# All sixteen decodes of second-layer weights during the first layer, and the second output layer of group 0 as seven products

## The chip, the core and the metric

The kernel runs on one core of one Trainium2 chip. The metric is device time in microseconds (us) of the whole kernel. Work is shared by TensorE (PE, matrix products), VectorE (DVE), ScalarE (ACT), GpSimd (POOL), and SyncE (SP), which here only issues DMAs, in order, from one queue.

## The reference

All values are float32. Attention without a softmax is followed by a normalisation and by two layers with a hidden dimension:

```
kv  = einsum('bhsd,bhse->bhde', k, v);  o = einsum('bhsd,bhde->bhse', q, kv)      # 8 x 8 heads x 576 x 64
x   = o / sqrt(mean(o*o, -1) + 1e-6) * g_norm          # reshaped to 4608 tokens x 512
x   = (sigmoid(x @ w_gate) * (x @ w_val)) @ w_out      # 512 -> 1536 -> 512, first layer
h   = x @ w_in                                         # 512 -> 2048, second layer
out = where(h > 0, h, exp(min(h, 0)) - 1) @ w_out2     # 2048 -> 512
```

## The kernel before

Precision. Each float32 factor is split into a high and a low half, and a product of two factors is three matmuls into one PSUM bank (high x high, high x low, low x high). For the activations of an output layer this is `split`: ACT writes the high half (line 725), DVE the low half (line 727), into one of three buffers J.

Tiling. The 4608 tokens are six groups of two blocks of 384. For every group in turn the first layer runs its input stage (gate and value products) and its output stage; the attention of the group after is woven in between. Then for every group in turn the second layer runs its input stage (`in2`, line 846 on) and its output stage. Results of the first layer wait in DRAM (x2d).

Seven products. A product of 2 x 2 blocks is done as seven block products instead of eight, on sums and differences of blocks, with additions of PSUM banks into SBUF afterwards. `quad` does that for input stages. For the output stage of the second layer there are two functions: `out2_plain` keeps six PSUM banks and streams 512 columns per matmul; `out2` makes the differences T1, T2, T3 of the input blocks (`combine`, line 891, on POOL, the last of each on DVE; T4 on DVE), runs seven products of 256 columns per matmul (lines 916 to 918) and adds up on DVE (line 930). Group 0 takes `out2_plain`, the other five `out2`. The T buffers of `out2` ("w") lie in the memory of the buffers raw, wk and kv.

Weights. The second layer's weights arrive in a packed form and are decoded on the chip, sixteen times (eight pairs of tiles for the input layer, "I", eight for the output layer, "O"). A decode loads two raw tiles (line 359, 512 KB each), makes words on ACT (lines 362, 364) and DVE (366, 370), builds four sums on POOL (378 to 381) in a buffer sf, splits both into halves (ACT 385, DVE 386), and stores the pieces to DRAM (wsI, wsO; lines 395 and 398). All later products read these pieces into five buffers S of 1 MB. Twelve decodes run in the first layer, as the tuple `DEC` deals them to groups 0 to 5; the four that are left run in group 0 of the second layer, marked `late`. A late decode takes its sf from the three kv buffers, which until group 5 of the first layer hold the attention's k and v loads (line 499); the others take it from the four wk buffers.

Order. All work is written down as tasks with dependencies. The order on PE is that of the program; the orders on DVE, ACT, POOL and SP come from a planner (`Plan`), which places tasks by due times and tries random variations from a seed. Engines then run their lists in order, so a row that waits holds up all rows behind it.

Of the kernel before, what the change touches and what calls it, by code (L numbers as in the profile page):

```python
# [32 lines left out]
WARM = 7  # L33
IDLE = (8, 8, 20, 40)
LAG = 4.0
DEC = (0,2,3,3,2,2)
SEVEN = (1,2,3,4,5)


# [25 lines left out]
class Plan:  # L65
# [16 lines left out]
    def add(self, eng, dur, fn, after=(), bufs=(), due=None, queue=None):  # L82
        t = Task(eng, dur, fn, after, bufs, due, len(self.tasks))
        for d in t.after:
            d.next.append(t)
        self.tasks.append(t)
        if eng == "PE":
            (self.pe if queue is None else queue).append(t)
        return t
# [22 lines left out]

    def run(self):

        tries, now, rand = [], 0.0, random.Random(3)
        for t in self.pe:
            t.started, now = now, now + t.dur
        cuts = [0] + self.marks + [len(self.pe)]

        def one(times, bias={}):  # L120
            for t in self.tasks:
                t.bias = bias.get(t, 0.0)
            for t, x in zip(self.pe, times):
                t.started = x
            if len(self.round()) < len(self.tasks):
                return times
            got = [t.started for t in self.pe]
            end = max(t.started + t.dur for t in self.pe)
            tries.append((end, times, got, [(got + [end])[b] - got[a] for a, b in zip(cuts, cuts[1:])], bias, [t.started for t in self.tasks]))
            return got  # L130

        times = [t.started for t in self.pe]
        for n in range(self.ROUNDS):
            got = one(times)
            times = [(x + y) / 2 for x, y in zip(times, got)] if n % 2 else got
        for n in range(self.MIXES):
            mixed, at = [], 0.0
            for k, (a, b) in enumerate(zip(cuts, cuts[1:])):
                r = min(tries, key=lambda r: r[3][k])
                wide = rand.choice((0.0, 0.5, 1.5, 4.0, 8.0)) if n else 0.0  # L140
                mixed += [x - r[1][a] + at + rand.uniform(-wide, wide) for x in r[1][a:b]]
                at += r[3][k]
            one(sorted(mixed))
        busy = [sum(t.dur for t in self.pe[a:b]) for a, b in zip(cuts, cuts[1:])]
        for n in range(self.STEPS):
            best = min(tries, key=lambda r: r[0])
            k = rand.choices(range(len(busy)), [x - y + 0.3 for x, y in zip(best[3], busy)])[0]
            a, b = cuts[k], cuts[k + 1]
            if n % 3:
                lo, hi = (best[2] + [best[0]])[a] - 5.0 if k else 0.0, (best[2] + [best[0]])[b]  # L150
                wide, bias = rand.choice((1.0, 3.0, 8.0)), dict(best[4])
                for t, x in zip(self.tasks, best[5]):
                    if t.eng != "PE" and lo <= x < hi and rand.random() < 0.08:
                        bias[t] = rand.uniform(-wide, wide) if rand.random() < 0.8 else 0.0
                one(best[1], bias)
                continue
            other = rand.choice(sorted(tries, key=lambda r: r[3][k])[:8]) if n % 2 else best
            wide = rand.choice((0.3, 1.0, 3.0, 6.0))
            shift = (best[2] + [best[0]])[a] - (other[2] + [other[0]])[a]
            now = [x + shift + rand.uniform(-wide, wide) for x in other[1][a:b]]  # L160
            one(sorted(best[1][:a] + now + best[1][b:]), best[4])
        for t in self.tasks:
            t.bias = min(tries, key=lambda r: r[0])[4].get(t, 0.0)
        for t, x in zip(self.pe, min(tries, key=lambda r: r[0])[1]):
            t.started = x
        order = self.round()
        assert len(order) == len(self.tasks)
        return order
# [123 lines left out]
def tile_kernel(ctx: ExitStack, tc: tile.TileContext, kv, kvtail, qt, g2, w1, w2, out):  # L292
# [5 lines left out]
    plan = Plan()  # L298
# [51 lines left out]
    def decode(layer, fp, after=None, late=False):  # L350

        src, idx = (w1, "gvo".index(layer)) if layer in "gvo" else (w2, "IO".index(layer))
        order = (2 * fp, 2 * fp + 1) if layer in "oO" else (2 * fp + 1, 2 * fp)
        k = "3" if late else "2" if layer in "IO" else ""
        wh, wp = plan.buf("wk", "wh" + k), plan.buf("wk", "wp" + k)
        word = []
        for n, f in enumerate(order):
# [4 lines left out]
            a = add("ACT", 0.57, lambda raw=raw, n=n: nc.scalar.activation(  # L362
                wh.slot[:, n, :], raw.slot[:, :, 1].bitcast(F32), AF.Copy, scale=2.0 ** -112), [ld], [raw, wh])
            b = add("ACT", 0.57, lambda raw=raw, n=n: nc.scalar.activation(
                wp.slot[:, n, :].bitcast(I32), raw.slot[:, :, 0].bitcast(U32), AF.Copy, scale=0.93 * 2.0 ** -29), [ld], [raw, wp])
            c = add("DVE", 0.61, lambda raw=raw, n=n: nc.vector.scalar_tensor_tensor(
                wp.slot[:, n, :].bitcast(I32), raw.slot[:, :, 1], -(2 ** 31), wp.slot[:, n, :].bitcast(I32),
                op0=ALU.bitwise_and, op1=ALU.bitwise_or), [b], [raw, wp])
# [3 lines left out]
            op0=ALU.logical_shift_left, op1=ALU.bitwise_or), word, [wh, wp])  # L372
        if layer in "IO":
            d = ws2[fp] if layer == "I" else wo2[:, :, fp]
            sf = plan.buf("kv", "kv", "q a c n -> q a (c n)") if late else plan.buf("wk", "sf")
            A = lambda i: (wh.slot[:, i // 2, i % 2 * 256:i % 2 * 256 + 256] if layer == "I" else wh.slot[:, i % 2, i // 2 * 256:i // 2 * 256 + 256])
            T = lambda i: sf.slot[:, i // 2, i % 2 * 256:i % 2 * 256 + 256]
            s1 = add("POOL", 0.72, lambda: nc.gpsimd.tensor_tensor(T(0), A(0), A(1), op=ALU.add), [w], [wh, sf])
# [460 lines left out]
    def load_x2(g, blk):  # L839
        res = []  # L840
        for m in range(NCC):
            f = plan.buf("v", "xf")
            res.append((f, dma(P * BLK * 4, lambda f=f, m=m: nc.sync.dma_start(out=f.slot, in_=x2d[g][:, blk, m, :]), [x2_there[g, blk, m]], [f], early=40.0)))
        return res
# [153 lines left out]
    n = len(plan.tasks)  # L998
# [8 lines left out]
    for fp in range(2):  # L1007
        dec[fp] = decode("g", fp) + decode("v", fp)
    rate[0] = 340e3
    hs = [{} for _ in range(NF1 // 2)]  # L1010
# [31 lines left out]
    for fp in range(NF1 // 2):  # L1042
        dec[fp] = decode("o", fp)
    w2_pairs = [(c, fp) for c in "IO" for fp in range(NF2 // 2)]
    for g in range(NG):
        if g:
# [3 lines left out]
            hs = [in1(fp, X, done, fresh if g == 1 else stream) for fp in range(NF1 // 2)]  # L1050
# [3 lines left out]
        n = len(plan.pe)  # L1054
        plan.marks.append(n)
        (out1_products if g in SEVEN else out1)(g, hs)
        if g:
            m = DEC[g]
            a, b = n if g == 1 else start + 30, n - 20 if g > 1 else len(plan.pe) - 20
# [4 lines left out]
    for g in range(NG):  # L1064
        plan.marks.append(len(plan.pe))
        X, done = sides(load_x2(g, 0), load_x2(g, 1), "DVE")
        n = len(plan.pe)
        hs = [in2(fp, X, done) for fp in range(NF2 // 2)]
        if g == 0:
            m = len(w2_pairs)  # L1070
            for k in range(m):
                decode(*w2_pairs.pop(0), after=plan.pe[n + int((len(plan.pe) - n) * (0 + (0.8 - 0) * k / m))], late=True)
            gate = add("POOL", 0.05, lambda: None, [t for t in plan.tasks if any(b.cls in ("raw", "wk", "kv") for b in t.bufs)])
        (out2 if g else out2_plain)(g, hs)

    for t in plan.run():
        t.fn()
# [31 lines left out]
```

## Time and profile before

| | |
|---|---|
| median of 3 runs | 1631.77 us (1631.62 to 1632.13) |
| profiled execution, own time | 1632.44 us |
| its span, first to last instruction | 1630.7 us |
| PE busy | 1617.9 us, 99% of the span |
| DVE busy | 1197.0 us, 73% |
| ACT busy | 854.6 us, 52% |
| POOL busy | 427.4 us, 26% |
| DMA moved | 495.27 MB, mean 304 GB/s |
| granted TensorE clock | 1.0 in the mean |

The busy share of an engine is an average over stages. Matmuls are pipelined, their records overlap, and a busy PE need not stream at its peak; the length of a stage over its count of matmuls says what one costs. An idle time is put down to the releaser that came last. "SPq" rows are DMAs that SP issues. A DMA's share is the mean busy share of the core's 16 DMA engines.

### The profile page before, as it was taken

Reading aid. Unit: us, or ns where it says so; the run is one execution under the profiler, and the core shown is the slowest. Engines: PE = TensorE matmul, PEld = TensorE weight load, DVE = VectorE, ACT = ScalarE, POOL = GpSimd, SP = SyncE. Lnnn points to the kernel's source line nnn. Section 1 sums busy time; section 2 is a strip of 40 time slices with the busy share of each in tenths; the row PEclk is TensorE's granted clock in tenths of the full one; section 3 lists DMA queues with packets and bytes.
Section 4 is the critical chain, followed back from the end, with each engine's and each line's share of the span. In section 5 each row is a group of like instructions: output and inputs, shape, how many; then the busy total and the mean of one; then the engine's idle time right before and its main releaser. Section 6 shows DMA issues by size and latency. Waiting matters only on the chain.

```text
span 1630.7 us, 29131 instructions
## 1 busy us (share of the span) xinstructions
PE 1617.9 (99%) x10655; PEld 1586.2 (97%) x10655; DVE 1197.0 (73%) x2228; ACT 854.6 (52%) x1731; POOL 427.4 (26%) x418
## 2 busy tenths in 40 slices
PE   8999999999999999999999999999999999999999
PEld 7999999999999999999999998999999999999999
DVE  5869777955885696689458878578668679578666
ACT  5567434633553364455235665466556466465564
POOL 0005578023403412440352012230220320320310
PEclk9999999999999999999999999999999999999999
DMA  9987899899889899989988999878778778678774
GB/s 359 361 306 255 317 343 331 312 356 327 318 299 358 310 345 345 324 325 304 337 322 314 322 350 307 286 273 298 246 278 286 264 275 292 238 290 293 249 280 154
DMA packets 145408, 495.27 MB, mean 304 GB/s; under 512 B 12528, under 2 KB 70384, under 8 KB 118000
## 3 DMA queue, kind: packets, MB, share of 16 engines
q1 hardware_dynamic: 145264, 493.41, 85.3%
q8 instruction: 84, 1.38, 0.3%
q14 instruction: 60, 0.49, 0.1%
HBM read 402.13 MB, written 91.23 MB: 303 GB/s over the span
## 4 chain that ended last, share of the span: by engine, by line
PE 90%; DVE 7%; DMA 1%; issue 1%; ACT 1%; DVEq 0%; ACTq 0%; SPq 0%
PE psi L489 20%; PE psi L490 20%; PE psi L491 20%; PE psi L918 4%; PE psi L917 4%; PE psi L916 4%; DVE J L727 3%; PE psa L491 3%; PE psa L489 3%; PE psa L490 2%; PE psa L563 2%; PE psa L917 2%; PE psa L916 2%; PE psa L918 2%; PE psa L526 1%; PE psa L607 1%
## 5 line engine op out<-in xcount | busy, mean ns | idle before, releaser
L659 DVE TENSOR_TENSOR v<-v,psi 128x384 f32<-128x384 f32 x540 | 297.7, 551 | 198.1 <-PE psi L491 178.5
L489 PE MATMUL psi<-x,S 128*128 128x384 f32 x1056 | 356.8, 338 | 0.1
L490 PE MATMUL psi<-x,S 128*128 128x384 f32 x1056 | 353.0, 334 | 0.9 <-DVE x L616 0.9
L491 PE MATMUL psi<-x,S 128*128 128x384 f32 x1056 | 353.0, 334 | 0.0
L725 ACT ACTIVATE J<-v 128x384 fp32r<-128x384 f32 x426 | 222.3, 525 | 181.6 <-PE psa L491 89.5
L727 DVE TENSOR_TENSOR J<-v,J 128x384 fp32r<-128x384 f32 x426 | 250.4, 598 | 56.6 <-ACT J L725 55.0
L489 PE MATMUL psi<-xt,S 128*128 128x384 f32 x648 | 218.2, 337 | 0.1
L491 PE MATMUL psi<-xt,S 128*128 128x384 f32 x648 | 216.5, 334 | 0.0
L490 PE MATMUL psi<-xt,S 128*128 128x384 f32 x648 | 216.5, 334 | 0.0
L489 PEld LDWEIGHTS psi<-x,S 128*128 128x128 f32 x1056 | 198.3, 188 | 2.5 <-DVE v L659 0.9
L490 PEld LDWEIGHTS psi<-x,S 128*128 128x128 f32 x1056 | 198.4, 188 | 1.4 <-DVE x L616 1.2
L491 PEld LDWEIGHTS psi<-x,S 128*128 128x128 f32 x1056 | 198.3, 188 | 0.0
L695 POOL TENSOR_TENSOR v<-v,v 128x384 f32<-128x384 f32 x90 | 103.6, 1158 | 317.5 <-DVE v L659 279.6
L918 PE MATMUL psi<-S,J 128*128 128x256 f32 x560 | 159.0, 284 | 0.6 <-DVE J L727 0.5
L916 PE MATMUL psi<-S,J 128*128 128x256 f32 x560 | 158.4, 283 | 0.0
L917 PE MATMUL psi<-S,J 128*128 128x256 f32 x560 | 158.4, 283 | 0.0
L851 ACT ACTIVATE v<-v 128x384 f32<-128x384 f32 x144 | 75.2, 522 | 113.1 <-DVE v L659 112.9
L853 DVE SCALAR_TENSOR_TENSOR v<-v,v 128x384 f32<-128x384 f32 x144 | 91.4, 636 | 52.9 <-ACT v L852 52.9
L489 PEld LDWEIGHTS psi<-xt,S 128*128 128x128 f32 x648 | 121.7, 188 | 1.4 <-DVE v L659 1.0
L490 PEld LDWEIGHTS psi<-xt,S 128*128 128x128 f32 x648 | 121.7, 188 | 0.0
L491 PEld LDWEIGHTS psi<-xt,S 128*128 128x128 f32 x648 | 121.6, 188 | 0.0
L663 ACT ACTIVATE v<-psi 128x384 f32<-128x384 f32 x108 | 52.4, 485 | 125.7 <-PE psi L491 125.1
(170 smaller groups left out, 3434.2 us busy)
## 6 DMA issues: line engine op xcount, KB each, us to landing
S<-wsO SPq DMA_DIRECT2D x78, 1024.0 KB, 7.1
S<-wsI SPq DMA_DIRECT2D x48, 1024.0 KB, 5.5
S<-wsI SPq DMA_DIRECT2D x48, 768.0 KB, 5.6
S<-wso SPq DMA_DIRECT2D x35, 1024.0 KB, 6.5
raw<-w SPq DMA_DIRECT2D x68, 512.0 KB, 6.1
S<-wsg SPq DMA_DIRECT2D x24, 1024.0 KB, 7.1
S<-wsv SPq DMA_DIRECT2D x24, 1024.0 KB, 7.3
S<-wsg SPq DMA_DIRECT2D x30, 768.0 KB, 6.6
```

The source lines that it names most:

```text
L489: nc.tensor.matmul(acc, wh, xh, start=first, stop=False, skip_group_check=more)
L490: nc.tensor.matmul(acc, wh, xl, start=False, stop=False, skip_group_check=more)
L491: nc.tensor.matmul(acc, wl, xh, start=False, stop=last, skip_group_check=more)
L659: return add("DVE", T_DVE, lambda: nc.vector.tensor_tensor(dst.slot, a.slot, bank[k].slot[:, :BLK], op=ALU.add), after, [dst, a, bank[k]])
L695: t = add("POOL", T_POOL, lambda r=r, b=b: nc.gpsimd.tensor_tensor(r.slot, r.slot, b.slot, op=ALU.mult), [d, s], [r, b])
L725: hi = add("ACT", T_ACT, lambda: nc.scalar.activation(j.slot[:, 0, :], f.slot, AF.Copy), [d], [j, f])
L727: lo = add("DVE", T_DVE, lambda: nc.vector.tensor_tensor(j.slot[:, 1, :], f.slot, j.slot[:, 0, :].bitcast(F32), op=ALU.subtract), [hi], [j ...
L851: a1 = add("ACT", T_ACT, lambda e=e, b=b: nc.scalar.activation(e.slot, ps_or_v(b), AF.Relu, scale=-1.0), [d], [e, b])
L853: res[int(n[0]) - 1, int(n[1]) - 1] = (e, add("DVE", T_DVE, lambda e=e, b=b: nc.vector.scalar_tensor_tensor(e.slot, e.slot, -1.0, ps_or_v( ...
L916: nc.tensor.matmul(acc, x[0], w[:, 0], start=st, stop=False, skip_group_check=True)
L917: nc.tensor.matmul(acc, x[0], w[:, 1], start=False, stop=False, skip_group_check=True)
L918: nc.tensor.matmul(acc, x[1], w[:, 0], start=False, stop=last and f == n - 1, skip_group_check=True)
```

## The change

`DEC` now adds up to sixteen, so no decode is left for the second layer, and every decode takes its sf from the kv buffers, with names ("wh3", "wp3") that no cap limits. Group 0 of the second layer calls `out2` like the others. The planner's seed goes from 3 to 4.

```diff
-DEC = (0,2,3,3,2,2)
+DEC = (0,3,4,3,3,3)
...
-        tries, now, rand = [], 0.0, random.Random(3)
+        tries, now, rand = [], 0.0, random.Random(4)
...
-        k = "3" if late else "2" if layer in "IO" else ""
+        k = "3" if layer in "IO" else ""
...
-            sf = plan.buf("kv", "kv", "q a c n -> q a (c n)") if late else plan.buf("wk", "sf")
+            sf = plan.buf("kv", "kv", "q a c n -> q a (c n)")
...
-        (out2 if g else out2_plain)(g, hs)
+        out2(g, hs)
```

The planner deals the order of every engine anew. Three places follow.

POOL, from the last decode's sums to the first differences of an output stage. Before, these first differences are those of group 1 (rows of line 891; v are blocks of activations; raw, wk and kv the memory that the T buffers use):

```order
L380 TENSOR_TENSOR kv_145<-kv_145,wk_142 128x256
L381 TENSOR_TENSOR kv_145<-wk_142,kv_145 128x256
L891 TENSOR_TENSOR raw_136<-v_126,v_120 128x384
L891 TENSOR_TENSOR raw_136<-v_114,raw_136 128x384
L891 TENSOR_TENSOR v_126<-v_114,v_126 128x384
L891 TENSOR_TENSOR raw_137<-v_85,v_118 128x384
L891 TENSOR_TENSOR raw_137<-v_100,raw_137 128x384
L891 TENSOR_TENSOR v_85<-v_100,v_85 128x384
```

Now they are those of group 0:

```order
L380 TENSOR_TENSOR kv_144<-kv_144,wk_142 128x256
L381 TENSOR_TENSOR kv_144<-wk_142,kv_144 128x256
L891 TENSOR_TENSOR raw_136<-v_120,v_80 128x384
L891 TENSOR_TENSOR raw_136<-v_105,v_117 128x384
L891 TENSOR_TENSOR raw_137<-v_125,v_121 128x384
L891 TENSOR_TENSOR raw_137<-v_111,v_106 128x384
L891 TENSOR_TENSOR raw_138<-v_124,v_84 128x384
L891 TENSOR_TENSOR raw_138<-v_98,v_81 128x384
L891 TENSOR_TENSOR wk_139<-v_127,v_94 128x384
L891 TENSOR_TENSOR wk_139<-v_83,raw_136 128x384
```

Before, T1, T2 and T3 of one pair of blocks follow each other; now seven of T1 come first, then seven of T2 (the last row shown is the first), then seven of T3.

SP, at the start of the second layer's output stage of group 0. The S rows from wsO are weight loads, the wsO rows from wk or kv are stores of decoded pieces. Before:

```order
L483 DMA S_131<-wsI_176 128x1536 [waits DMAHW1_49,PE_49]
L480 DMA S_128<-wsO 128x4x512 [waits DMAHW2_49,PE_49]
L398 DMA wsO<-wk_140 128x2x256 [waits DMAHW3_49]
L398 DMA wsO<-wk_142 128x2x256 [waits DMAHW4_49,DVE_49]
L480 DMA S_129<-wsO 128x4x512 [waits DMAHW6_49,DMAHW5_49,PE_49]
L480 DMA S_132<-wsO 128x4x512 [waits PE_49]
```

Now:

```order
L484 DMA S_128<-wsI_176 128x2048 [waits DMAHW4_49,DMAHW2_49,PE_49]
L904 DMA S_129<-wsO 128x2048 [waits DMAHW3_49,PE_49]
L398 DMA wsO<-wk_139 128x2x256
L398 DMA wsO<-wk_142 128x2x256 [waits DMAHW5_49]
L398 DMA wsO<-wk_142 128x2x256 [waits DMAHW6_49]
L904 DMA S_130<-wsO 128x2048 [waits DMAHW7_49,PE_49]
L904 DMA S_132<-wsO 128x2048 [waits DMAHW4_49,DMAHW6_49,DMAHW0_49,PE_49]
```

The stores that were spread over the whole output stage now end behind its first weight load; PE reads S_129 first, then S_132, whose load waits for the stores (DMAHW4, DMAHW6), and then S_130.

SP, in the input stage of the first layer's group 2, where the attention's k and v are loaded into the kv buffers. Before:

```order
L483 DMA S_129<-wsv_166 128x1536 [waits DMAHW1_49,PE_49]
L499 DMA kv_145<-kv 128x1024 [waits DMAHW2_49,PE_49]
L483 DMA S_131<-wsg_161 128x1536 [waits DMAHW3_49]
L359 DMA raw_137<-w 128x1024 [waits DMAHW4_49,DVE_49]
L484 DMA S_130<-wsg_161 128x2048 [waits DMAHW5_49,PE_49]
```

Now:

```order
L484 DMA S_130<-wsv_166 128x2048 [waits DMAHW1_49,PE_49]
L499 DMA kv_143<-kv 128x1024 [waits DMAHW2_49,PE_49]
L499 DMA kv_144<-kv 128x1024 [waits DMAHW3_49,PE_49]
L483 DMA S_128<-wsg_161 128x1536 [waits DMAHW4_49]
L484 DMA S_131<-wsg_161 128x2048 [waits DMAHW5_49,PE_49]
```

Two k and v loads now wait for PE's matmuls on the pair before, where one did.

## Rows read from the trace of the kernel before

**Rows 1.** Windows view by stage; first layer's output stages of groups 2, 5; second layer's.
```profile
core 0: us, PE busy (x) PEld busy (x) DVE busy (x) ACT busy (x) POOL busy (x), PEclk, DMA share, GB/s
...
440.40:485.60 45.20, 44.45 (x253) 43.64 (x253) 41.24 (x78) 26.22 (x50) 6.44 (x6) 1.00 0.90 313
...
861.10:907.80 46.70, 44.33 (x254) 43.57 (x253) 42.22 (x80) 28.01 (x56) 7.12 (x6) 1.00 0.88 301
907.80:966.10 58.30, 58.30 (x339) 58.30 (x338) 44.88 (x84) 38.23 (x79) 2.88 (x4) 1.00 0.98 340
966.10:1031.40 65.30, 65.30 (x289) 54.05 (x289) 47.88 (x74) 36.67 (x68) 12.69 (x12) 1.00 0.95 322
...
1208.50:1270.40 61.90, 61.29 (x507) 60.68 (x506) 49.32 (x102) 35.56 (x73) 0.00 (x0) 1.00 0.84 291
...
1328.60:1389.10 60.50, 60.50 (x507) 60.50 (x506) 49.47 (x102) 36.31 (x74) 0.00 (x0) 1.00 0.85 297
```

**Rows 2.** Waits view of PE after 24 us: us in total, times, longest.
```profile
PE psi L490 <- DVE J L727: 3.8, 6, 1.7
```

**Rows 3.** Windows view by DMA share: groups 2, 3 and 4, then busy stretches.
```profile
323.80:470.40 146.60, 146.27 (x998) 143.69 (x997) 101.35 (x205) 66.78 (x142) 41.53 (x41) 1.00 0.92 327
470.40:758.90 288.50, 287.25 (x1826) 282.31 (x1825) 216.04 (x419) 137.85 (x275) 95.57 (x94) 1.00 0.94 331
...
190.00:250.00 60.00, 60.00 (x423) 58.36 (x423) 39.76 (x68) 22.92 (x45) 40.48 (x46) 1.00 0.98 361
340.00:400.00 60.00, 60.00 (x485) 58.39 (x484) 33.50 (x66) 22.98 (x53) 22.09 (x22) 1.00 0.96 348
```

**Rows 4.** SP's timeline near 951 us, and landings of DMAs issued from 951 to 962.
```profile
951.72 0.37 SPq L480 DMA_DIRECT2D S<-wsO  x1
...
S<-wsO SPq DMA_DIRECT2D x3, 1024.0 KB, 7.9
...
wsO<-wk SPq DMA_DIRECT2D x3, 256.0 KB, 8.3
wsO<-wk SPq DMA_DIRECT2D x1, 512.0 KB, 10.8
```

**Rows 5.** POOL's timeline: start, duration; beside a busy DVE (865, 1088) and alone.
```profile
865.93 1.05 POOL L379 TENSOR_TENSOR wk<-wk 128x256 f32<-128x256 f32 x1
...
942.75 0.74 POOL L379 TENSOR_TENSOR kv<-wk 128x256 f32<-128x256 f32 x1
...
1041.53 1.01 POOL L891 TENSOR_TENSOR raw<-v,v 128x384 f32<-128x384 f32 x1 [37.71 <-DVE v L853]
...
1088.66 1.34 POOL L891 TENSOR_TENSOR v<-v,v 128x384 f32<-128x384 f32 x1
```

**Rows 6.** DVE's timeline at the start of group 5's output stage, and later in it.
```profile
863.16 3.22 DVE L727 TENSOR_TENSOR J<-v,J 128x384 fp32r<-128x384 f32 x3
...
881.03 0.55 DVE L639 TENSOR_TENSOR x<-v,x 128x384 fp32r<-128x384 f32 x1
881.50 0.55 DVE L774 TENSOR_TENSOR v<-v,v 128x384 f32<-128x384 f32 x1
```

**Rows 7.** PE's timeline in group 5's output stage: start, duration, idle before and releaser.
```profile
869.46 0.45 PE L490 MATMUL psi<-J,S 128*128 128x384 f32 x1 [1.66 <-DVE J L727]
```

**Rows 8.** Lines of DVE that a decode runs: busy us, mean ns.
```profile
L366 DVE SCALAR_TENSOR_TENSOR wk<-raw,wk 128x512 int32<-128x512 int32 x68 | 50.2, 746 | 21.4 <-ACT wk L364 21.2
...
L370 DVE SCALAR_TENSOR_TENSOR wk<-wk,wk 128x1024 int32<-128x1024 int32 x34 | 43.9, 1291 | 4.2 <-ACT wk L362 3.4
...
L386 DVE TENSOR_TENSOR wk<-wk,wk 128x1024 fp32r<-128x1024 f32 x28 | 35.0, 1252 | 3.4 <-ACT wk L385 2.7 <-ACT J L725 0.8
```

**Rows 9.** SP's and PE's timelines and a DMA landing: k and v in group 2.
```profile
389.75 0.33 SPq L499 DMA_DIRECT2D kv<-kv  x1
...
397.86 1.15 PE L526 MATMUL psa<-kv 128*64 128x64 f32 x32
...
kv<-kv SPq DMA_DIRECT2D x2, 512.0 KB, 8.5
```

## The prediction

> **What bounds the kernel now.** I began with the page: PE is busy 99% of the span, the granted clock is full in all 40 slices, and the chain that ended last is 90% PE. So time goes away only if PE gets less to stream or sits idle less. Next I cut the span into stages with the windows view [rows 1]. The output stage of group 0 in the second layer, the one that the change rewrites, takes 65.30 us for 288 matmuls of 512 columns and PE is never idle in it. The same stage of groups 2 and 3, already written as seven products, takes 61.90 and 60.50 us. Then the waits of PE [rows 2]: after the start it waits almost only for the low half of a split input (J, line 727, on DVE), 3.8 us in six waits, all in the first layer. No wait of PE for a DMA is in that view. But the windows show what stands close behind: DVE is busy 41 to 42 us of every 45 to 47 in the first layer's output stages [rows 1], and DMA runs at a share of 0.92 to 0.94 through groups 2 to 4 [rows 3]. The change must be judged against both.
>
> **What it removes.** 288 matmuls of 512 columns become 504 of 256. From stage length over count, one of 512 costs 65.30 / 288 = 0.2267 us and one of 256 60.50 / 504 = 0.1200 us [rows 1]. The records of single matmuls overlap, so they can't be summed. The gain is 65.3 - 60.5 = **4.8 us** if group 0 runs as group 3 does. Four decodes leave group 0 of the second layer; PE is not idle there (58.30 of 58.30 and 65.30 of 65.30 us busy [rows 1]), so their going is worth nothing by itself.
>
> **What it adds at the place of the gain.** The seven products need 24 differences of input blocks (T1, T2, T3), 21 of them on POOL. In the later groups POOL does all of them during the input stage: it is busy 0.00 us in the output windows of groups 2 and 3 [rows 1]. In group 0 they can't be that early. The order shows why: POOL has seven of T1, then seven of T2, then seven of T3, instead of one of each per block, and the seventh of T1 goes into the buffer wk_139, whose last store SP issues behind the first weight load of the output stage. In the trace that load is issued at 951.72 us, and a 256 KB store near it lands after 8.3 us [rows 4], so the seventh T1, with 14 operations behind it, starts at about 961. The output stage starts at 966.1. At 1.01 us alone and 1.3 us against a busy DVE [rows 5], the fifteen last until about 980, and some ten of them stand beside the first splits.
>
> What that costs PE I take from the one place where it already happened, the start of the output stage of group 5. POOL's small operations there (0.74 us alone) took about 1.05 us each, and DVE's work on two SBUF inputs slowed from 0.47 us a piece (start to start, 881.03 to 881.50) to 1.07: three splits in 3.22 us [rows 5, 6]. PE then waited 1.66 us [rows 7]. With an operation of 1.01 us in place of 0.74 a split comes every 1.07 + 0.27 = 1.34 us (an estimate from these rows). PE uses one up in 9 x 0.120 = 1.08 us. That is 0.26 us lost per split, 2.6 us over ten. The three J buffers give a lead that takes some of it off, the few DVE operations left over from the input stage, slowed too, put some on. Scaling the 1.66 us by POOL's time (10 x 1.3 = 13 us against 7.1 in that window [rows 1]) gives 3.0. I take **+2.8**. Lower end 0 (T differences done before 966 after all); upper end 15 x 0.26 and two of the leftovers 0.87 us late each (1.34 - 0.47), 5.6. The value lies nearer the middle because the same pairing cost 1.66 us already.
>
> The Trainium skill (SBUF — State Buffer, section "SBUF: two separate sides") speaks against the change here: DVE with two SBUF inputs and GpSimd hold a shared port pair exclusively for a whole instruction, the other fully blocks. Taken at its word with this trace's lengths, a split would come every 1.01 + 0.47 = 1.48 us, 0.4 us lost each, 4.0 over ten, and the sum below would be 1.2 us higher. The rows of group 5 show a little overlap (1.07, where 0.74 + 0.47 is 1.21), so I stay with 2.8.
>
> **A wait on SP at the same place.** In the new order the two last stores of decoded pieces stand right behind the first weight load (951.72), and the third weight load, the second half of the first product's weights, waits for them. Stores issued by 952.7 land at 961.0 (8.3 us [rows 4]; a 512 KB one took longer, 10.8); the load then takes 7.9, so 968.9. Its first use is after four splits, 966.1 + 4 x 1.08 = 970.4. **0**, at worst 1.0.
>
> **What it adds to the first layer.** Four decodes move there, one each to groups 1, 2, 4 and 5. A decode reads 1.05 MB and writes 1.8 to 2.1. Summing the sizes of SP's rows from one input stage's first weight load to the next: group 2 goes from 47.9 to 50.7 MB, groups 3 and 4 together from 94.6 to 99.2, group 5 from 44.4 to 44.8 (its late stores slip into the second layer). Over the same stretches of the trace, 146.6 and 288.5 us, that needs 346 and 344 GB/s, where 327 and 331 were moved at shares of 0.92 and 0.94 [rows 3]. In proportion the share becomes 0.98. Two stretches of 60 us at 348 and 361 GB/s and shares of 0.96 and 0.98 exist, with PE never idle in them [rows 3]. So I expect the weight loads to stay hidden, with **+0.6** for a late one; ends 0 and 12 (the rival below). DVE gets 2 x 0.75 + 1.3 + 2 x 1.25 = 5.3 us per decode, by the means of these lines [rows 8]; over a stage of some 145 us that fits, and in the output stages the order has about as many clusters of DVE work between splits as before.
>
> The sums of a decode now sit in a kv buffer, one of three that the attention's k and v loads share. So in groups 2, 3 and 4 both loads of the second pair wait for PE's first pair, not one. Before, the load issued at 389.75 was used at 397.86, 8.1 us later; a pair issued together took 8.5 to land [rows 9]. The gaps in groups 3 and 4 are 10 to 11 us long. **+0.4**, between 0 and 1.2.
>
> **What is dealt anew.** The order of every engine changes with the planner's seed, so the existing idle spots (2.4 us in group 5's output stage, 0.75 in group 2's, 0.6 in the second layer's group 2 [rows 1]) move. In group 5 the new order has fewer DVE operations among its first splits, in group 3 there is one larger cluster. **-0.5**, between -3 and +2.
>
> **Sum.** -4.8 + 2.8 + 0 + 0.6 + 0.4 - 0.5 = -1.5 us. The profiled execution took 1632.44 us (1630.7 of span and 1.7 around it): 1630.9. The runs' median is 0.67 lower, 1631.77, so the forecast is **1630.3 us**. About 0.2%, 3.3 us, is what a measurement can tell from no change: below 1628.5 is faster, above 1635.0 slower.
>
> **Rivals.**
> *The gain comes whole.* POOL gets through T1 to T3 beside DVE operations that read PSUM and need no waiting, or DVE catches up out of its idle 0.5 us per split later. For it: 6.4 us of POOL work in the output window of the first layer's group 2 go with only 0.75 us of idle PE [rows 1]. Against: here it is twice as much, all of it beside splits. -4.8 + 0.6 + 0.4 - 0.5 = -4.3, 1627.5 us; with idle spots gone as well, 1625.5. Chance 0.30.
> *The blocking is worse.* Ten splits at 1.48 us, two leftovers 0.87 us late each and the SP wait of 1.0 behind them: -4.8 + 4.0 + 1.7 + 1.0 + 0.6 + 0.4 = +2.9, 1634.7 us. By the rule quoted above this is half true at least. Chance 0.13.
> *DMA becomes the bound in groups 2 to 4; this one ends slower.* 149.9 MB (50.7 + 99.2) have to pass in 435.1 us. If the mix with the decodes' small packets can't be held above 335 GB/s, that takes 447.5 us: +12.4 - 4.8 + 2.8 = +10.4, 1642 us. Of the gain 2.0 us are left by then (4.8 - 2.8), so it decides against the change below 149.9 / (435.1 + 2.0) = 343 GB/s; at 340 PE loses 5.8 us and the time is 1635.6. Against: [rows 3] hold 348 and more, though only for 60 us at a time, and PE waits for no DMA today. Chance 0.12.
> *The change does nothing of its own:* excluded, since PE's order has the 504 matmuls and no 512-column ones.
> The forecast, 1628.5 to 1633, has 0.45.
>
> **Range and chances.** Faster: the whole gain and a small part of the forecast's lower edge, 0.33. Slower: most of the DMA case and the upper edge of the worse blocking, 0.13. Same: 0.54. The range, 1626.2 to 1635.0, leaves out the best of the whole gain and most of the DMA case, some 2 in 10. The likeliest case has 1628.5 to 1633.
>
> **What the next profile would show.** Right: 504 matmuls of 256 columns from about 966 to 1029; POOL's line 891 still running 10 us and more into that window; splits there at 1.2 us and longer, PE waiting for line 727 by 2 to 4 us in the stage's first 15 us; PE waits for DMA under 1 us; DMA share 0.96 to 0.98 in groups 2 to 4. Wrong: a group 0 output window of 60.5 us; or PE idle on S<-wsg or S<-wso loads; or idle spots in the first layer's output stages that differ by more than 2 us from today's.

## The result and the profile after

The changed kernel takes **1640.31 us** (median of four runs, 1639.49 to 1641.10), the kernel before 1631.69 beside it (1631.15 to 1632.13): ratio 1.0053, 95% interval 1.0041 to 1.0065. It is slower by 8.6 us, where 1.5 us less was forecast, and lies above the range.

First the windows of the changed kernel, which answer to [rows 1]: output stages of groups 2, 4 and 5 of the first layer, then both stages of group 0 and the output stage of group 2 in the second.

```profile
core 0: us, PE busy (x) PEld busy (x) DVE busy (x) ACT busy (x) POOL busy (x), PEclk, DMA share, GB/s
445.40:490.40 45.00, 44.69 (x253) 43.53 (x253) 44.95 (x80) 27.94 (x52) 10.29 (x10) 1.00 0.95 333
736.50:784.30 47.80, 45.59 (x253) 43.38 (x253) 45.63 (x82) 28.83 (x56) 6.57 (x6) 1.00 0.96 317
871.70:916.00 44.30, 43.99 (x253) 43.58 (x252) 39.18 (x78) 28.20 (x57) 1.85 (x2) 1.00 0.95 327
916.00:976.10 60.10, 59.11 (x338) 58.08 (x337) 48.17 (x84) 39.03 (x81) 16.66 (x18) 1.00 0.94 331
976.10:1040.30 64.20, 62.65 (x505) 60.99 (x505) 57.66 (x102) 36.54 (x74) 15.13 (x13) 1.00 0.83 290
1217.00:1277.50 60.50, 60.50 (x505) 60.50 (x504) 49.56 (x102) 36.34 (x74) 0.00 (x0) 1.00 0.83 296
```

The clock is full in these stages. The rewritten stage went from 65.3 to 64.2 us, not to 60.5. Group 5's output stage gained 2.3 us and group 2's in the second layer 1.4, both places where a new order was expected to move idle spots. But group 4's output stage has 2.2 us of idle PE, and group 0's input stage in the second layer, which was free of idle time before, has 1.0.

PE's waits after 27 us answer to [rows 2].

```profile
PE psi L490 <- DVE J L727: 4.4, 9, 1.0
PE psi L489 <- DVE v L659: 3.2, 6, 1.0
PE psi L918 <- DVE J L727: 1.6, 2, 1.1
```

Still no wait for a weight load. New are the waits for line 659, DVE's sums of PSUM in the input stages, whose banks PE wants back. At the very start there are two more, 1.9 us and 0.8 us, for k and v. Behind the longer one the granted clock is 0.50, the lower of its two levels (1.2 instead of 2.4 GHz), from 11.93 to 15.34 us; the kernel before is at 1.00 there. The window, then the first matmuls behind the wait, then the same ones before:

```profile
11.93:15.34 3.41, 3.41 (x30) 2.62 (x31) 1.60 (x3) 1.49 (x3) 0.00 (x0) 0.50 1.05 394
```

```profile
11.90 1.12 PE L526 MATMUL psa<-wk 128*64 128x64 f32 x16 [1.92 <-DMA wk<-kv]
```

```profile
10.10 0.69 PE L526 MATMUL psa<-wk 128*64 128x64 f32 x16
```

From there to the next k and v matmuls PE took 4.70 us (11.90 to 16.60), before 3.16 (10.10 to 13.26): the lower clock cost 1.5 us.

For all later comparisons I cut each trace where PE starts the first matmul of a stage. This table, worked out from one trace of each, has stage lengths in us ("1.out4" is the output stage of group 4 in the first layer) for the kernel before, the changed one, and five kernels described below ("quiet": fourteen of the sixteen decodes without their DVE and POOL work). Stages left out agree within 0.2.

```
stage      before   changed  before,   before s4  changed   changed,   changed,
                             seed 4    quiet      quiet     DVE quiet  POOL quiet
start       23.67    26.61    23.06     24.57      26.42     27.87      26.64
1.in0      121.09   120.52   122.42    122.84     120.18    120.42     120.88
1.out0      49.93    49.93    50.57     50.55      49.92     49.92      49.92
1.in1       99.71   101.15    99.16     99.16     101.11    101.08     101.26
1.out1      43.72    44.27    43.82     43.81      44.32     44.24      44.24
1.in2      102.28   102.92   102.28    102.28     102.74    102.74     102.96
1.out2      45.22    45.01    45.41     44.78      44.45     46.13      44.65
1.in3       98.91    98.91    98.64     98.65      99.05    100.17      98.95
1.out3      44.73    46.37    45.53     44.80      45.73     47.49      46.31
1.in4       99.40   100.82    99.19     99.16      99.52     99.51     100.27
1.out4      44.96    47.80    44.63     44.27      45.30     47.58      47.25
1.in5       87.54    87.36    87.47     87.45      87.36     87.36      87.36
1.out5      46.69    44.36    44.22     44.22      44.36     44.35      44.38
2.in0       58.24    60.08    58.24     58.24      58.24     58.91      59.19
2.out0      65.32    64.24    65.32     65.32      63.60     64.24      64.24
2.out2      61.87    60.47    60.47     60.47      60.46     60.46      60.47
from 1.out0 to the end of the last matmul, sum
          1482.09  1487.18  1478.23   1476.44    1479.64   1487.64    1484.92
```

From before to changed the start with its input stage costs +2.4, group 1 +2.0, group 2 +0.4, group 3 +1.6, group 4 +4.3 and the second layer's first input stage +1.8; group 5 gives -2.5, the rewritten stage -1.1, the rest -1.5. The sum is some +7.5 us, for spans of 1638.3 and 1630.7.

### The profile page after: what moved, and what is told of

It reads as the page before. It is cut to its first block, busy times and chain, and to the rows that moved or that the text cites. A ratio compares the mean times of both kernels' runs of the same rounds, so it can differ in the third digit from the quotient of the medians.

```text
span 1638.3 us, 29755 instructions
## 1 busy us (share of the span) xinstructions
PE 1618.6 (99%) x10871; PEld 1592.6 (97%) x10871; DVE 1231.0 (75%) x2273; ACT 866.9 (53%) x1753; POOL 450.1 (27%) x439
## 4 chain that ended last, share of the span: by engine, by line
PE 87%; DVE 9%; DMA 1%; issue 1%; ACT 1%; SPq 0%; DVEq 0%; ACTq 0%
PE psi L489 19%; PE psi L490 19%; PE psi L491 18%; PE psi L918 5%; PE psi L916 5%; PE psi L917 5%; DVE J L727 3%; PE psa L918 2%; PE psa L917 2%; PE psa L916 2%; PE psa L563 2%; PE psa L491 2%; PE psa L490 2%; PE psa L489 2%; DVE v L659 1%
## 5 line engine op out<-in xcount | busy, mean ns | idle before, releaser
L727 DVE TENSOR_TENSOR J<-v,J 128x384 fp32r<-128x384 f32 x426 | 257.8, 618 | 44.8 <-ACT J L725 42.7
L918 PE MATMUL psi<-S,J 128*128 128x256 f32 x672 | 191.2, 284 | 1.6 <-DVE J L727 1.6
L916 PE MATMUL psi<-S,J 128*128 128x256 f32 x672 | 190.2, 283 | 0.0
L917 PE MATMUL psi<-S,J 128*128 128x256 f32 x672 | 190.1, 283 | 0.0
L695 POOL TENSOR_TENSOR v<-v,v 128x384 f32<-128x384 f32 x90 | 98.3, 1098 | 272.7 <-DVE v L659 233.6
L918 PEld LDWEIGHTS psi<-S,J 128*128 128x128 f32 x672 | 128.9, 192 | 3.2 <-DVE J L727 3.0
L916 PEld LDWEIGHTS psi<-S,J 128*128 128x128 f32 x672 | 128.9, 192 | 0.0
L917 PEld LDWEIGHTS psi<-S,J 128*128 128x128 f32 x672 | 128.9, 192 | 0.0
L489 PEld LDWEIGHTS psi<-xt,S 128*128 128x128 f32 x648 | 121.7, 188 | 3.4 <-DVE v L659 2.7
```

What stands on the lines that cost most here:

```text
L489: nc.tensor.matmul(acc, wh, xh, start=first, stop=False, skip_group_check=more)
L695: t = add("POOL", T_POOL, lambda r=r, b=b: nc.gpsimd.tensor_tensor(r.slot, r.slot, b.slot, op=ALU.mult), [d, s], [r, b])
L727: lo = add("DVE", T_DVE, lambda: nc.vector.tensor_tensor(j.slot[:, 1, :], f.slot, j.slot[:, 0, :].bitcast(F32), op=ALU.subtract), [hi], [j ...
L916: nc.tensor.matmul(acc, x[0], w[:, 0], start=st, stop=False, skip_group_check=True)
L917: nc.tensor.matmul(acc, x[0], w[:, 1], start=False, stop=False, skip_group_check=True)
L918: nc.tensor.matmul(acc, x[1], w[:, 0], start=False, stop=last and f == n - 1, skip_group_check=True)
```

## The experiments

**Is it the new deal of the planner?** The kernel before with the changed kernel's seed alone, and the changed kernel with the old seed and with a third.

```diff
-        tries, now, rand = [], 0.0, random.Random(3)
+        tries, now, rand = [], 0.0, random.Random(4)
```

> The kernel before with the planner's seed 4 and nothing else changed. Theory A (the new deal of the orders is what costs: 2.4 us at the start, and PE's waits for DVE in the first layer's stages, +5.8 us there in the changed kernel): slower than before by 3 to 8 us, with the late k and v load at the start in it. Theory B (the four decodes moved into the first layer cost it, whatever the order): within 1.5 us of before, and of the start's 2.4 us only what belongs to the seed.

Measured 1629.43 us (ten runs, 1629.18 to 1630.36), ratio 0.9987 [0.9978, 0.9996]. So the seed is worth -2 us by itself (its table column shows group 5 and 2.out2), and the rest of the change costs 11 us against this kernel, which beats both others. Theory A falls.

> The changed kernel with the planner's seed left at 3. Theory A (the deal costs): it gets back most of 8.6 us, 1631 to 1634 us, and the start's 2.4 us are gone. Theory B (the moved decodes cost, whatever the order): 1637 to 1641 us, first-layer stages again 4 to 7 us longer in all than before. Both: the output stage of group 0 in the second layer near 64 us if POOL's differences run into it, since that does not hang on the seed.

Measured 1645.53 us, ratio 1.0091 [1.0076, 1.0106], 5.2 us above the changed kernel. One row of PE's waits is more than that:

```profile
PE psa L526 <- DMA kv<-kv: 6.7, 1, 6.7
```

This is the second k/v pair of group 2, whose input stage is 10 us longer (112.50): SP issues one load of the pair at 392.82 us, the other at 402.66, when PE already stands, and PE goes on at 408.36, with the clock at 0.50 from 403.81 to 414.05. It is the place of the prediction's "sums of a decode now sit in a kv buffer", priced at 0.4, and absent with seed 4.

> The change with the planner's seed 5, a third deal. Theory 'the moved decodes cost some 7 us in any deal, of which the seven products give back about 1': 1636 to 1646 us, slower than before; second layer's output stage of group 0 at 64 us. Rival 'seeds 4 and 3 were poor deals': under 1632.

Measured 1643.17 us, ratio 1.0068 [1.0051, 1.0085]; 2.out0 63.60. Three deals, three slower kernels.

**Which part of the change?** Sixteen decodes in the first layer, but group 0 by the plain product:

```diff
-        out2(g, hs)
+        (out2 if g else out2_plain)(g, hs)
```

> The changed kernel (seed 4, sixteen decodes in the first layer), but group 0's second output layer as the plain function again. The order is dealt anew by this too. Theory B: the first layer stays 4 to 7 us longer than before and the output stage takes 65.3 us, so 1637 to 1642 us in all. Theory A: first layer within 2 us of before in this other deal, 1630 to 1634 us.

Measured 1638.66 us, ratio 1.0043 [1.0026, 1.0060], with 65.32 us in 2.out0. Moving the decodes, with their new buffers, costs 7 us without the seven products. Then the buffers: `sf` back in a wk buffer with the old cap, in the changed kernel; and the kernel before, seed 4, with `sf` in kv and without the cap.

```diff
-        k = "3" if layer in "IO" else ""
+        k = "2" if layer in "IO" else ""
-            sf = plan.buf("kv", "kv", "q a c n -> q a (c n)")
+            sf = plan.buf("wk", "sf")
```

> The changed kernel (seed 4, sixteen decodes in the first layer, seven products), but a decode takes its sums' buffer from the wk buffers and the old caps hold, as the first-layer decodes of before did. Theory C (sharing the kv buffers with the attention's loads, and decodes that no cap holds apart, is what costs): most of the 8.6 us come back, 1631 to 1634 us. Theories A (the decodes' work on DVE) and B (their DMA traffic): 1637 to 1643 us, no wait of PE for k and v, but the waits for DVE remain.

Measured 1667.32 us, ratio 1.0219 [1.0204, 1.0235]. The decodes finish late: 2.out0 takes 79.8 us, where PE waits 9.3 us for weight loads and the clock is at 0.50 for 20 us (993.85 to 1014.33).

> The kernel before with seed 4 (1629.4 us) and one edit: all its decodes take the sums' buffer from kv, without caps. Twelve decodes stay in the first layer and group 0 keeps the plain function. Theory C: 1633 us or more, with waits of PE for k and v or for DVE. Theories A and B: 1628.5 to 1631 us.

Measured 1633.16 us (ten runs, 1631.43 to 1634.71), ratio 1.0008 [0.9999, 1.0018]: 3.7 us above the same seed without it, as Theory C forecast (1633 or more). In its trace 2.7 us of this lie behind 1.out0 (1480.94 in place of 1478.23). But the order is dealt anew here, and no run parts that from the buffers. So the shared kv buffers stay a possible part of the cost; the old buffers cannot hold sixteen decodes in time.

**The rewritten stage.** POOL's fourteen operations of T2 and T3 for group 0 left out, the order kept:

```diff
-                t = add(on, t, lambda e=e, d=d, a=a, b=b: ...
+                t = add(on, t, (lambda: None) if g == 0 and on == "POOL" and whole is not B12 else lambda e=e, d=d, a=a, b=b: ...
```

> The changed kernel with the same order on all engines, but without the fourteen POOL operations that make T2 and T3 of the second layer's group 0; the products then read other data of the same shape, so part of the output is not computed. If POOL beside the splits is what makes the output stage of that group 64.2 us long, splits there come every 1.08 us from the start and the stage takes 60.5 to 61.0 us, the whole 3.2 to 3.8 us less. Rival: late weight loads or late inputs make it long; then it stays near 64 us.

Measured 1636.96 us (one run), 2.out0 60.60 us instead of 64.24. The predicted collision is what takes the gain. Without these operations a split takes 0.56 us, one comes every 1.08 us, and DVE is idle before each:

```profile
983.80 0.56 DVE L727 TENSOR_TENSOR J<-v,J 128x384 fp32r<-128x384 f32 x1 [0.52 <-ACT J L725]
```

In the changed kernel's own trace DVE's splits and POOL's line 891 stand like this, DVE first:

```profile
978.73 1.36 DVE L727 TENSOR_TENSOR J<-v,J 128x384 fp32r<-128x384 f32 x1
980.02 1.36 DVE L853 SCALAR_TENSOR_TENSOR v<-v,v 128x384 f32<-128x384 f32 x1
981.30 11.29 DVE L727 TENSOR_TENSOR J<-v,J 128x384 fp32r<-128x384 f32 x10
```

```profile
972.28 1.26 POOL L891 TENSOR_TENSOR wk<-v,v 128x384 f32<-128x384 f32 x1 [6.02 <-DVE v L853]
973.50 7.46 POOL L891 TENSOR_TENSOR wk<-v,raw 128x384 f32<-128x384 f32 x6
980.93 1.31 POOL L891 TENSOR_TENSOR wk<-v,wk 128x384 f32<-128x384 f32 x1
982.20 9.04 POOL L891 TENSOR_TENSOR v<-v,v 128x384 f32<-128x384 f32 x7
```

While POOL runs, until 991.2, a split comes every 1.28 us where PE needs one per 1.08; of the ten in the last row only the two behind POOL's end come 0.47 us apart. The seventh T1 starts at 972.28 because its input block comes late (released by line 853), not because of a store.

**Two repairs.** In the changed kernel's order, two raw loads at the start were moved behind the k/v loads that use wk buffers, and each T3 of group 0 went right behind the T1 of its block.

```diff
+        if cls == "wk":
+            first_kv.append(ld)
+    for t in raws[:2]:
+        move.append((t, first_kv[1]))
+    for i in range(7):
+        t, to = early_t["T3", i], early_t["T1", i]
+        move.append((t, max([to] + list(t.after), key=lambda d: at[d])))
```

> The change in its own order but for two places: the first two loads of raw words go behind the two early k/v loads that use wk buffers, and on GpSimd each of seven T3 stands right behind the T1 of its block. Theory: the start's late k/v loads cost 2.4 us or more and the late T operations beside the splits 3.8 us, of which 6 of 15 operations leave the place; start back to about 24 us, output stage of group 0 in the second layer 62.5 to 63 us in place of 64.2: 1635 to 1637 us. Rival 'what leaves the start comes back in the next stage, and the splits lose their time to GpSimd whatever stands there': under 1.5 us, 1639 or more.

Measured 1640.01 us (1637.38 to 1641.47), ratio 1.0050 [1.0035, 1.0065]: both stages improved as expected (start 24.96, with the clock full; 2.out0 62.99), and the time hardly did, as the rival had it (1639 or more). In the profiled execution, the slowest of the four (1641.47), 1.in0 took 1.1 back, 1.out3 and 1.out4 took 2.0. Where about half of the 2.0 comes from is seen below, in the run with DVE quiet. In another attempt the planner's price for DVE's decode instructions was raised:

```diff
-            c = add("DVE", 0.61, ...
+            c = add("DVE", 0.61 if layer not in "IO" else 1.2, ...
-        w = add("DVE", 1.14, ...
+        w = add("DVE", 1.14 if layer not in "IO" else 2.0, ...
-                l = add("DVE", 1.14, ...
+                l = add("DVE", 1.14 if layer not in "IO" else 2.0, ...
```

> The change, with the planner's cost of VectorE's instructions in the sixteen decodes raised from 0.61 and 1.14 us to 1.2 and 2.0; a new deal comes with it. If the planner then keeps them out of the tight output stages, those stages of groups 2 to 4 lose 2 to 4 us and the time is 1634 to 1637; if the buffers and due times fix where the decodes go, the output stages stay at 1638 to 1644 us in all, or the decodes come late.

Measured 1643.63 us (one run). 1.out3 and 1.out4 fall to 43.95 and 44.90, but 1.out2 rises to 48.23, 1.in1 to 104.33 and 2.in0 to 62.69. In 1.in1 and in 2.in0 PE waits 2.2 and 2.3 us for line 659 and the clock is at 0.50 for 3.4 us behind it. This deal wins nothing in sum. One stage is telling, though: here POOL does T1, T2 and T3 block by block from 962 us on and ends at 981.4, before the output stage begins at 982.2, and 2.out0 takes 60.57 us. The whole 4.75 us is to be had in this stage when POOL is done before it; here the stage before it lost nearly as much (62.69 for 58.24), most of it in the wait just named and behind it.

**DMA.** The kernel before with seed 4 and 24 additional copies of 512 KB from DRAM to DRAM, each issued behind a raw load (12.6 MB more in the first layer):

```diff
-            ld = dma(P * DM * 8, lambda raw=raw, f=f: nc.sync.dma_start(
-                out=raw.slot..., in_=src[f, :, idx].bitcast(I32)), [after], [raw])
+            ld = dma(P * DM * 8, lambda raw=raw, f=f: [nc.sync.dma_start(
+                out=raw.slot..., in_=src[f, :, idx].bitcast(I32))] + ([nc.sync.dma_start(
+                out=spare_copy[layer, f], in_=src[f, :, idx].bitcast(I32))] if layer in "IO" and not late else []), [after], [raw])
```

> The kernel before with seed 4 (1629.4 us) and its order, and for each of the 24 raw loads of the first layer's decodes a second DMA of 512 KB from DRAM to DRAM: 12.6 MB more, as much as the four moved decodes bring, and no work on any engine. Theory B: groups 2 to 5 of the first layer get 3 to 8 us longer in all. Theories A and C: within 1.5 us, at DMA shares near 0.97.

Measured 1630.0 us (one run), all stages behind the start as without the copies. The windows over about groups 2, 3 with 4, and 5, then groups 2 and 3 with 4 of the changed kernel:

```profile
338.00:486.00 148.00, 147.10 (x1000) 143.91 (x999) 105.32 (x207) 70.70 (x146) 46.32 (x45) 1.00 0.97 360
485.00:773.00 288.00, 287.07 (x1826) 282.40 (x1825) 212.13 (x416) 135.26 (x272) 91.97 (x90) 1.00 0.95 345
773.00:907.00 134.00, 133.93 (x771) 133.17 (x770) 93.02 (x167) 56.07 (x109) 42.12 (x42) 1.00 0.97 352
```

```profile
342.40:490.40 148.00, 147.57 (x998) 143.50 (x997) 115.60 (x215) 74.30 (x152) 54.44 (x53) 1.00 0.96 345
490.40:784.30 293.90, 289.03 (x1825) 281.97 (x1825) 226.04 (x425) 142.39 (x283) 94.73 (x94) 1.00 0.97 339
```

360, 345 and 352 GB/s pass with PE idle 0.9, 0.9 and 0.1 us in these windows, as without the copies; the changed kernel moves less in groups 2 to 4 (345 and 339). The bytes are not the cause. The small packets of the decodes' stores were not added here; they are all in the run with fourteen quiet decodes below, which gets most of the time back.

**The decodes' work on DVE and POOL.** Four decodes (two of each kind) without it, order kept:

```diff
+        keep = (layer, fp) not in (("I", 2), ("I", 6), ("O", 4), ("O", 7))
+        only = lambda fn: fn if keep else lambda: None
```

> The changed kernel with its order on all engines, but for four decodes (one each in groups 1, 2, 4 and 5, those that the change adds) the DVE and POOL instructions are left out; their DMAs, ACT work and buffers stay, and their pieces hold other data, so the output is not right in part. Theory A: the first layer and the second layer's first input stage get 3 to 6 us shorter, the whole 1634 to 1637 us. Theories B and C: within 1.5 us of the changed kernel.

Measured 1639.09 us (one run). Its start was 1.5 us longer with the same order; behind it 2.85 us came back, a little under the 3 to 6 of Theory A. So the same was done to fourteen decodes, in the changed kernel and in the kernel before with seed 4:

```diff
+        only = lambda fn: fn if layer not in "IO" or fp in (0,) else lambda: None
```

> The change in its own order; of the sixteen decodes of second-layer weights fourteen (all but the first of each kind) leave out their work on VectorE and GpSimd, while their loads and stores stay. Theory 'the decodes' work on VectorE and GpSimd is what the first layer cannot hide': four quiet ones gave 2.85 us in the stages behind the start; fourteen should give most of what the first layer lost, 6 to 10 us, so 1630 to 1634 us with a start as in the change. Rival 'it is the transfers and buffers, which stay': under 3 us, 1637 to 1640.

> The kernel before with the seed 4, in its own order; the same fourteen decodes leave out their work on VectorE and GpSimd. Reference for the run before it: if the decodes' work on those engines costs more in the new arrangement, as the theory says, less is won here, 1 to 4 us, 1625 to 1629 us. Rival 'the work costs the same in both arrangements': as much as in the other, 6 us or more, under 1624.

Measured 1632.0 and 1629.43 us (one run each). From 1.out0 to the end, where the start does not blur it, the decodes' work costs 1487.18 - 1479.64 = **7.5 us** in the changed kernel and 1478.23 - 1476.44 = **1.8 us** in the old arrangement. These 5.7 us are the larger part of the 9.0 between the two. But the 9.0 is net of what the rewritten stage wins: the other stages lose 10.0 us, 5.1 of them with the decodes' work and 4.9 without it. Of the 4.9, 1.9 are in 1.in1, where PE waits for line 659 behind other DVE work. Leaving out instructions also sets buffers free earlier; these runs do not part the two.

> The change in its own order; fourteen of the sixteen decodes leave out their work on VectorE alone, GpSimd's four operations of each stay. Theory 'VectorE's long decode instructions stand in front of splits and sums that PE waits for': 6 to 7.5 of the 7.5 us behind the start come back, stages behind the first input stage 1480 to 1481 us in sum (1487.2 in the change, 1479.6 with both engines quiet). Rival 'GpSimd's operations slow VectorE down': 1484 or more.

> As before, but only GpSimd's four operations of each of the fourteen decodes are left out, VectorE's work stays. Theory: 0 to 1.5 us come back, 1485.5 to 1487.5 in sum. Rival: 3 us or more, under 1484.

Measured 1641.69 and 1638.2 us (one run each); sums 1487.64 and 1484.92. DVE's part alone gives back **nothing** in sum, POOL's alone 2.3, both together 7.5. The nothing is a net: 1.in4 and 2.in0 give back 2.5 us, 1.out2, 1.in3 and 1.out3 take 3.5 (in 1.in3 PE waits 0.9 us for a weight load). The theory as written, that it is DVE's long instructions alone, falls; neither did the rival come in with its 3 us. What took the place of DVE's work stands in ACT's timeline of the kernel with DVE quiet:

```profile
612.60 0.67 ACT L365 ACTIVATE wk<-raw 128x512 int32<-128x512 uint32 x1 [1.84 <-DMA wsI<-wk]
613.17 0.51 ACT L726 ACTIVATE J<-v 128x384 fp32r<-128x384 f32 x1
...
770.62 0.66 ACT L365 ACTIVATE wk<-raw 128x512 int32<-128x512 uint32 x1 [2.19 <-DMA wsO<-wk]
771.18 0.51 ACT L726 ACTIVATE J<-v 128x384 fp32r<-128x384 f32 x1
```

and PE's beside the second (lines are one further down than in the changed kernel, 726 is its 725):

```profile
771.74 0.44 PE L490 MATMUL psi<-J,S 128*128 128x384 f32 x1 [0.46 <-ACT J L726]
```

ACT's next decode step may not overwrite a wk buffer before the stores of the last one have landed. It waits 2.2 us at the head of ACT's queue, the high half of the next split stands behind it, and PE waits. A matmul of these stages starts 0.173 us after the last one where nothing is late. By what exceeds that, PE loses 1.25 us right behind such waits in 1.out3 and 2.3 us in 1.out4; these stages are 1.8 and 2.3 us longer than with both engines quiet. In 1.out2 of this run it is POOL instead: its four sums (1.05 us each) start at 448.75, two splits beside them take 2.10 us, and PE waits twice. The same ACT wait, 1.61 us, ends at 609.78 and at 769.38 in the run with the two repairs, in the two stages that became longer there. Behind the first PE loses 1.0 us, behind the second nothing for 5 us. All this was read from the traces; no run took the wait itself away. It does not cost by itself either: between 190 and 980 us ACT waits some 20 us for such stores in the changed kernel and as long with fourteen decodes quiet.

## Why the prediction was wrong

**The gain** (-4.8) was right: 504 matmuls in 60.5 to 60.6 us wherever nothing is late.

**POOL beside the splits** (+2.8): the mechanism was right, the term too small; 64.24 - 60.47 = 3.8. PE's new splits follow each other by 1.28 us there (six of them, from 983.99 to 990.42 us; 1.34 was forecast). What weighs more is that the place opens with two waits, 0.42 and 1.13 us, from DVE operations slowed to 1.36 us before the lead was built; the prediction had such leftovers in its upper end only.

```profile
980.15 0.39 PE L918 MATMUL psi<-S,J 128*128 128x256 f32 x1 [0.42 <-DVE J L727]
982.71 0.38 PE L918 MATMUL psi<-S,J 128*128 128x256 f32 x1 [1.13 <-DVE J L727]
```

The rival "the gain comes whole" is what this stage shows in the deal of higher prices; that it did not happen here is a matter of when POOL's operations run. The Trainium skill's rule (SBUF — State Buffer, section "SBUF: two separate sides") gave, as an estimate with this trace's lengths, 1.48 us per split and a cost of 4.0. The spacing of 1.28 is against full exclusion, the sum of 3.8 is close to it.

**The wait on SP** (0) was right, PE waits for no load there. But the store that the seventh T1 was to wait for did not hold it; its input block did. That it began 3.8 us before the stage, where about 5 was forecast, is luck. **DMA** (+0.6) and its rival: right that weight loads stay hidden; where DMA does reach PE, as the traces read, it is by stores that ACT waits for. The rival's 1642 us is close to the result, but its mechanism is not what happened: there is no wait for weights, and more bytes pass freely.

**The k/v pair** (+0.4, to 1.2): 0 in this deal, a wait of 6.7 us in another. Its bound was taken from landing times; a load can also be issued late, and then nearly its whole latency shows.

**What failed** is the step "What it adds to the first layer", in its sentence "over a stage of some 145 us that fits, and in the output stages the order has about as many clusters of DVE work between splits as before", which priced four decodes' work at nothing. The stages are not alike: DVE is busy 44.95 of 45.00 us in group 2's output stage, and 39.18 of 44.30 in group 5's, where the new order put no decode instruction on DVE. DVE's time in lines 366, 370 and 386 inside the three output stages of groups 2 to 4, first before (three lines in that order), then after, from windows of these stages:

```profile
sum 134.90, DVE 4.13; mean DVE 1.38
sum 134.90, DVE 3.67; mean DVE 1.23
sum 134.90, DVE 4.90; mean DVE 1.63
```

```profile
sum 139.20, DVE 6.02; mean DVE 2.01
sum 139.20, DVE 4.88; mean DVE 1.63
sum 139.20, DVE 9.77; mean DVE 3.26
```

12.7 us became 20.7. The amount alone is not the price: by the same windows group 2's output stage got 6.3 us instead of 3.8 and became no longer (45.22, then 45.01). What counts is where the instructions stand, and that is plain in group 4's output stage, DVE first, then PE:

```profile
771.37 0.55 DVE L727 TENSOR_TENSOR J<-v,J 128x384 fp32r<-128x384 f32 x1
771.84 1.22 DVE L370 SCALAR_TENSOR_TENSOR wk<-wk,wk 128x1024 int32<-128x1024 int32 x1
772.97 1.55 DVE L727 TENSOR_TENSOR J<-v,J 128x384 fp32r<-128x384 f32 x2
```

```profile
764.18 0.45 PE L490 MATMUL psi<-J,S 128*128 128x384 f32 x1 [0.54 <-DVE J L727]
767.19 0.45 PE L490 MATMUL psi<-J,S 128*128 128x384 f32 x1 [0.65 <-DVE J L727]
773.58 0.45 PE L490 MATMUL psi<-J,S 128*128 128x384 f32 x1 [0.92 <-DVE J L727]
```

The second and the third wait follow a decode instruction of 1.2 us on DVE (the second line 386 at 765.44), the first comes out of three line-807 sums in a row; DVE has hardly any idle time around them in which to catch up. With fourteen decodes quiet the first wait is still there (0.54 us at 760.59), the other two are gone, and the stage takes 45.30 us. In all, the 7.5 us are 3.7 in the output stages of groups 2 to 4, 3.1 in 1.in4 and 2.in0, where PE waits for line 659, and 0.6 in 2.out0. So not the output stages alone were priced too low. The run with DVE quiet adds that DVE is not the decode's only limit: as its trace reads, ACT's wait for the stores and POOL's sums are close behind.

**"What is dealt anew"** (-0.5): the seed's own part was -2.2 (medians, 1629.43 for 1631.65), inside its bounds. The start, 2.4 us with its input stage, was not thought of: SP now issues two raw loads ahead of the k/v loads into wk buffers, the other way round than before, PE waits 1.9 us for those, and the lower clock behind the wait costs 1.5 more. How much of the 4.9 us that quiet decodes leave belongs to the deal and how much to sixteen decodes in kv buffers stays open.

Of the prediction's signs for "right", POOL's 15 us in the new stage, splits of 1.28 us and DMA shares of 0.96 and 0.97 came in. Of those for "wrong" one did, other idle spots in the first layer's output stages: group 5's has 2.1 us less idle PE, group 4's is 2.8 us longer.

## What to carry to other kernels

Work that is moved off a finished stage is not free where the average shows room: ask of each stage by itself how busy the receiving engines are, and count the moved instructions that land between the ones that the bound engine waits for. A chain over several engines through few buffers (load, ACT, DVE, POOL, store) has several limits close together; silence all of it once to learn what it costs at all, before mending one link. Read the granted clock behind each long wait: here the wait was not all that was lost. Compare orders that a planner dealt under the same seed and under several, since the seed alone was worth 2 us here and a buffer that is shared cost 0 in one deal and 6.7 in another.

## What the runs showed of the hardware

The DMA queues took 345 to 360 GB/s at a share of 0.95 to 0.97 over some 570 us without any stage behind the start becoming longer (the run with 24 copies). A DVE split with two SBUF inputs took 1.28 us start to start beside POOL operations (1.01 us alone), against 0.47 alone: most of the two lengths added up. In or right behind PE waits of 1.9 us (changed kernel, start), 2.3 us (higher prices, 2.in0) and 6.7 us (seed 3) the granted clock fell to 0.50, for 3.4, 3.4 and 10.2 us. The start of the kernel is the least repeatable part: in the six traces with the changed kernel's order of it, it took 26.4 to 28.1 us, with a wait for k and v of 1.9 to 3.1 us and the clock at 0.50 for 3.4 us in each.
